# Attention followed by an affine MLP on one core: k's first two heads loaded apart, q's second pair turned after the first scores, row work put further back

## The chip, the cores and the metric

The kernel runs on one core of one Trainium2 chip. The core has five engines that take their instructions each from its own queue, in order: TensorE (PE, with its weight loads shown apart as PEld), VectorE (DVE), ScalarE (ACT), GpSimd (POOL) and SyncE (SP). SyncE, ScalarE and GpSimd also issue DMA transfers. The metric is device time in microseconds. Three runs of the kernel before took 739.56, 739.91 and 741.48 us, the median being 739.91 us.

## The reference

Eight batches of grouped-query attention (16 query heads, 4 key and value heads, sequence 384, head dimension 64) feed a residual MLP over 1024 channels. Cut to what matters:

```python
k, v = np.repeat(k, 4, axis=1), np.repeat(v, 4, axis=1)
scores = np.matmul(q, k.transpose(0, 1, 3, 2)) / np.sqrt(64)
attn = softmax(scores)                       # over the last axis
x = np.matmul(attn, v).transpose(0, 2, 1, 3).reshape(8, 384, 1024)
a1 = alpha1 * x + beta1
tok = np.einsum('ts,bsd->btd', w_tok, a1)    # mixes tokens
u = x + lam * tok
a2 = alpha2 * u + beta2
out = u + lam * (np.maximum(a2 @ w_ch1, 0.0) @ w_ch2)   # 1024 -> 4096 -> 1024
```

Inputs and output are float32; the kernel multiplies in bfloat16.

## The kernel before

The bulk of the time goes to the channel MLP, whose weights stream through a ring of six chunks. The first two batches are done one by one (`main`), the other six in pairs. While TensorE works on the MLP of one batch, the attention of the next is woven in between. Only batch 0 has nothing to hide behind: its attention (`side(0)`) stands alone at the start of the program, and the change lies there.

The order on each engine is written by hand: within `tc.manual_schedule` the instructions of every engine stand in the order of the Python calls, and semaphores are put in where data or a buffer is waited for. `side(0)` builds a list `us` of calls. At its head stand the turns of the first heads, then follow 18 groups of scores; the dictionary `at` says what comes behind group `i`. A group covers four of the 72 blocks (8 head pairs with 9 blocks each), so pair 1 comes in with group 2 and pair 2, which needs key heads beyond head 0, with group 4.

The steps that matter:

- `warmup(n)`: n matmuls on a zeroed tile, whose results nobody reads. Nine stand at the start, behind the memset of `wtokT` on VectorE; three come behind score group 0 and one behind group 3.
- `load_k`: heads 0 and 1 of k as one 192 KB load on SyncE's queue, followed by the row loads (`load_row`) of alpha1 and lam, then heads 2 and 3, then the other rows. q's first two pairs are two loads on ScalarE's queue, its other heads come through GpSimd.
- `place_k(0, 0, hs)`: casts a head of k to bfloat16 and writes it twice, one copy by VectorE and one by ScalarE; heads 2 and 3 are cast by GpSimd (`place_k(0, 1)`).
- `k_transpose` and `q_transpose`: TensorE turns a head or a pair into a PSUM tile, and VectorE (for q's first pair ScalarE) copies it to `kT` or `qT`. The PSUM tiles are named by tags: "tp" and "av" have one buffer each, "sc" (scores) and "mm" two each.
- `scores(i)`: four matmuls (two for each half of the array) into an "sc" tile, and the exponential of the whole tile on ScalarE.
- `av(p)`: the product with v for pair p; VectorE divides by the row sums (`rinv`, then `x`).
- `scale_rows`, `split`, `spread`, `a1`: the row vectors alpha1 and lam are multiplied, split in two bfloat16 parts on VectorE (five instructions on 32 partitions), spread by TensorE over all partitions ("vec") and copied to `g1`; `a1(p)` multiplies pair p with it.
- `wtok_transpose`, `rows_r`, `tok`: the token weights are turned, the vector R is made from them, and the token mix follows.

Of the kernel before, what the change touches and what calls it, by code (L numbers as in the profile page):

```python
# [12 lines left out]
def kernel(  # L13
# [21 lines left out]
    nc = tc.nc  # L35
    f32 = mybir.dt.float32
# [7 lines left out]
    B, Hq, S, D = q.shape  # L44
    Hkv = k.shape[1]
# [3 lines left out]
    P = 128  # L49
    NST = S // P  # L50
# [30 lines left out]
    hTf = hT.rearrange("p n s -> p (n s)")  # L81
# [45 lines left out]
    wtokT = const.tile([P, NST, S], bf, tag="wtokT", name="wtokT")  # L127
# [5 lines left out]
    ks, k2s, qrs = {}, {}, {}  # L133

    def by_head(ap):
        return ap.rearrange("h (p st) d -> p h st d", st=NST)

    def k_tile(b):
        k2s[b] = sb.tile([P, Hkv, 2, NST, D], bf, tag="k2", name="k2", bufs=1)

    def load_k(b, hs=(0, 2)):
        if b > 1:
            k_tile(b)
            for a in range(2):
                nc.gpsimd.dma_start(out=k2s[b][:, :, a], in_=by_head(k[b]))
            return
        for h in hs:
            ks[b, h // 2] = t = hTf[:, 7680 + 384 * h:8448 + 384 * h].bitcast(f32).rearrange(
                "p (h st d) -> p h st d", h=2, st=NST)
            nc.sync.dma_start(out=t, in_=by_head(k[b, h:h + 2]))  # L150

    def place_k(b, i, hs=(0, 1)):
        if b not in k2s:
            k_tile(b)
        copies = [nc.gpsimd.tensor_copy] * 2
        if b == 1 or b == 0 == i:
            copies = (nc.vector.tensor_copy, nc.vector.tensor_copy if i else nc.scalar.copy)
        lo, hi = hs[0], hs[-1] + 1
        for a in range(2):
            copies[a](out=k2s[b][:, 2 * i + lo:2 * i + hi, a], in_=ks[b, i][:, lo:hi])  # L160
# [22 lines left out]
    def load_w1(c):  # L183
        w1_slots[c] = w1_free.pop(0)
        nc.gpsimd.dma_start(out=w1[:, w1_slots[c]], in_=w1src[:, :, c * CW * P:(c + 1) * CW * P])  # L185
# [5 lines left out]
    def bank(shape, tag, name, dtype=f32):  # L191
        if tag == "mm":
            return mms.tile(shape, dtype, tag="mm", name=name, bufs=2)
        return psum.tile(shape, dtype, tag=tag, name=name, bufs=2 if tag == "sc" else 1)
# [34 lines left out]
    def side(b):  # L229
# [172 lines left out]
        def add(f, *a):  # L402
            us.append(lambda: f(*a))
# [28 lines left out]
        if not first:  # L432
# [10 lines left out]
            if (b - NPL) // 2 > 0:  # L443
                at = {}
# [18 lines left out]
                **{39 + 4 * i - i // 2 * 2: [(turn, p)] for i, p in enumerate((5, 6, 7)) if by_pe(p)}}  # L463
        add(k_transpose, 0, 1)
        add(q_transpose, 0, 1, "av", "ACT")
        add(place_k, 0, 0, (1,))
        add(q_transpose, 1, 1, "tp")
        lower, upper = range(NP // 2), range(NP // 2, NP)
        ut = a2_transpose
        at = {0: [(warmup, 3), (scale_rows, 0), (split, 0, 1, 0)], 1: [(k_transpose, 1, 1)],  # L470
              2: [(q_transpose, 2, 2, "av"), (split, 0, 1, 1)], 3: [(warmup, 1)],
              4: [(av, 0)], 5: [(spread, lower, "tp"), (a1, 0)], 6: [(av, 1), (k_transpose, 2, 2, "tp")],
              7: [(q_transpose, 4, 2, "av"), (a1, 1)], 8: [(av, 2)],
              9: [(wtok_transpose, 0, "av"), (wtok_transpose, 1, "tp")],
              10: [(wtok_transpose, 2, "av"), (q_transpose, 6, 2, "mm"), (fill_h, 0)], 11: [(av, 3), (rows_r, "tp")],
# [363 lines left out]
    with tc.manual_schedule(engines=order):  # L839

        def warmup(n):
            warm = bank([P, 512], "mm", "warm")
            for _ in range(n):
                nc.tensor.matmul(out=warm[:, :S], lhsT=wtokT[:, 0, :P], rhs=wtokT[:, 1, :],
                                 start=True, stop=True)

        nc.vector.memset(wtokT, 0.0)
        warmup(9)
        load_k(0, [0])

        rows_f = hTf[:32, 9216:10496].bitcast(f32)
        rows_t = hTf[:32, 10496:11520].bitcast(f32)
# [15 lines left out]
        def load_row(i, ap, n=4):  # L868
            nc.sync.dma_start(out=rows_f[:n * NP, i * P:(i + 1) * P],
                              in_=bass.AP(tensor=ap.tensor, offset=ap.offset, ap=[[0, n], [P, NP], [1, P]]))  # L870

        load_row(0, moe_alpha1)
        load_row(3, moe_lam)
        load_k(0, [2])
        load_row(1, moe_beta1)
        load_row(2, moe_alpha2, 1)
        load_row(4, moe_beta2, 1)
# [5 lines left out]
        def load_q4(g):  # L883
            nc.gpsimd.dma_start(out=qgs[g], in_=q[0, g * G:(g + 1) * G].rearrange("h (p st) d -> p h st d", st=NST))
# [5 lines left out]
            nc.vector.memset(t[:, :, :, D:], 1.0)  # L890
        AX = mybir.AxisListType.X
        nc.vector.tensor_copy(out=ident_f, in_=ident)
        for i, m in enumerate(masks):
            nc.vector.tensor_reduce(out=m, in_=ident[:32, 8 * (i + 1):24 + 8 * (i // 2)], op=ADD, axis=AX)
        nc.vector.tensor_scalar(out=masks[2], in0=masks[2], scalar1=-1.0, scalar2=None, op0=MUL)
# [47 lines left out]
        load_q4(2)  # L943
        nc.gpsimd.dma_start(out=wtok_in, in_=moe_w_tok.rearrange("(p tt) s -> p tt s", tt=NST))
        load_q4(3)
        place_k(0, 0, (0,))
        load_w1(order1[0])
        load_w1(order1[1])
        place_k(0, 1)
        scale_rows(1, nc.gpsimd)  # L950
        split(1, 2, None, nc.gpsimd)
# [6 lines left out]
            load_w2(0, r, h)  # L958
        for i, f in enumerate(side(0)):
            f()  # L960
            if i == 3:
                load_k(1)
        for i in range(3):
            rows4.append(sb.tile([P, 512], f32, tag="es", name="rows4", bufs=EB))
# [14 lines left out]
        def put_flips(ps, phase, b, places):  # L979
            for u, m in zip(places, ((flip_k, b), *((flip_q, b, i, 2) for i in range(0, NP, 2)))):  # L980
                put(ps, phase, u, *m)

        turns, at = side(1)
        put_all(0, 0, turns)
        put_all(0, 1, at)
        put_flips(0, 1, 2, (34, 36, 37, 42, 43))

        put(0, 1, 45, load_next, 3)
        put_all(1, 0, side(2)[1], lambda u: int(1.5 * u))
        put_flips(1, 0, 3, (53, 55, 57, 59, 61))  # L990
        put_all(1, 1, side(3)[1])
# [68 lines left out]
```

## Time and profile before

| what | value |
|---|---|
| median of three runs | 739.91 us |
| the profiled execution, its own time | 739.61 us |
| its span, first to last instruction | 737.8 us |
| TensorE busy | 727.0 us (99% of the span) |
| VectorE busy | 512.0 us (69%) |
| ScalarE busy | 325.7 us (44%) |
| GpSimd busy | 164.0 us (22%) |
| first matmul of k's turn | 4.38 us |
| first score matmul | 5.91 us |
| first exponential | 6.34 us |

The span counts from the first to the last instruction, and the remaining 1.8 us of the time lie around it. In a timeline a line gives start and duration in microseconds, the engine, the line of the code, the operation, output and inputs with their shapes, how many instructions were merged into the line, and in brackets the idle time of the engine ahead of it with what ended that idle time. A merged line spans from its first start to its last end, and consecutive instructions overlap by some hundredths of a microsecond, because an engine begins one while the one before drains. The matmul of a turn is short, and what its consumer sees is later by the way through the array.

### The profile page before, as it was taken

The page shows a single profiled execution, that of the slowest core. Times are in us where ns is not written, and L with a number is a line of the kernel's source. Part 1 is how long each engine was busy: PE and PEld are TensorE (multiplying, and loading weights), DVE is VectorE, ACT ScalarE, POOL GpSimd, SP SyncE. Part 2 cuts the span into 40 slices and gives each one's busy share as a digit, 9 for nine tenths or more (in the row PEclk, how much of TensorE's full clock was granted, in tenths as well). Part 3 has the DMA queues.
Part 4 walks back from the last instruction along what each step waited for, and adds up shares of the span by engine and source line. Part 5 has one row for each costly group of instructions (what it writes and reads, how often), then busy time and mean ns, then how long its engine had stood idle before and what let it go on. Part 6 is the DMA issues. An engine that isn't in the chain of part 4 may idle for free.

```text
span 737.8 us, 14477 instructions
## 1 busy us (share of the span) xinstructions
PE 727.0 (99%) x5710; PEld 418.6 (57%) x5769; DVE 512.0 (69%) x993; ACT 325.7 (44%) x469; POOL 164.0 (22%) x211
## 2 busy tenths in 40 slices
PE   8999999999999999999999999999999999999998
PEld 5866555666555566655555566655555556654444
DVE  7763366467587889749777988747958988762354
ACT  7632431554332566663334366664343266660000
POOL 9434221420000332301012244020002222000011
PEclk9999999999999999999999999999999999999999
DMA  9999999999999999999979999998989999837965
GB/s 188 194 202 200 207 217 179 186 198 181 219 264 260 183 226 223 249 262 215 284 186 224 178 176 165 190 250 199 276 236 167 217 149 144 149 136 241 289 184 107
DMA packets 218017, 151.31 MB, mean 205 GB/s; under 512 B 88661, under 2 KB 197061, under 8 KB 217949
## 3 DMA queue, kind: packets, MB, share of 16 engines
q0 software_dynamic: 120304, 64.60, 66.8%
q1 hardware_dynamic: 96956, 85.33, 41.5%
q8 instruction: 45, 0.74, 0.4%
q10 hardware_dynamic: 688, 0.46, 0.2%
q14 instruction: 24, 0.19, 0.1%
HBM read 154.84 MB, written 38.27 MB: 262 GB/s over the span
## 4 chain that ended last, share of the span: by engine, by line
PE 85%; DVE 6%; DMA 5%; issue 2%; POOL 2%; ACT 0%; DVEq 0%; POOLq 0%
PE C L789 25%; PE X L723 17%; PE h L532 10%; PE ch L570 10%; PE Y L723 8%; PE sc L279 4%; PE Z L723 4%; PE sc L315 3%; PE sc L340 3%; DMA q_raw<-in_q_dram 2%; DMA ops<-a 1%; DMA out_dram<-hT 1%; DVE xr L323 1%; DVE hT L826 1%; DVE xr L347 1%
## 5 line engine op out<-in xcount | busy, mean ns | idle before, releaser
L288 ACT ACTIVATE es<-sc 128x1024 bf16<-128x1024 f32 x126 | 121.4, 1024 | 154.6 <-PE sc L279 143.5
L789 PE MATMUL C<-w,arena 128*128 128x512 bf16 (+2 forms) x711 | 163.7, 372 | 1.6 <-issue 0.3
L789 PEld LDWEIGHTS <-arena 128*128 128x128 bf16 x1040 | 94.8, 98 | 100.5 <-issue 5.1
L728 ACT ACTIVATE hT<-X,bias 128x384 f32<-128x384 f32 x144 | 83.8, 582 | 63.8 <-PE X L723 56.8
L723 PEld LDWEIGHTS <-w 128*128 128x128 bf16 x768 | 75.1, 98 | 50.5 <-issue 0.7
L185 POOL DMA_DIRECT2D w<-in_moe_w_ch_dram x68 | 62.2, 926 | 125.4 <-PE Z L723 51.7
L570 PE MATMUL ch<-arena,hT 128*128 128x512 bf16 x366 | 87.9, 379 | 1.0 <-issue 0.3
L517 POOL DMA_DIRECT2D out_dram<-hT x33 | 28.8, 872 | 258.4 <-DVE hT L688 79.7
L532 PE MATMUL h<-ops,w 128*128 128x384 bf16 (+1 forms) x480 | 83.2, 327 | 0.4
L723 PEld LDWEIGHTS <-pad 128*128 128x128 bf16 x576 | 56.4, 98 | 37.2
L723 PE MATMUL X<-ops,w 128*128 128x384 bf16 x384 | 70.2, 326 | 0.0
L723 PE MATMUL X<-ops,pad 128*128 128x384 bf16 x384 | 70.2, 326 | 0.0
L789 PE MATMUL C<-pad,arena 128*128 128x512 bf16 (+2 forms) x288 | 69.5, 373 | 0.4
L532 PEld LDWEIGHTS <-w 128*128 128x128 bf16 x480 | 45.3, 98 | 30.1 <-issue 1.8
L570 PEld LDWEIGHTS <-hT 128*128 128x128 bf16 x384 | 34.7, 98 | 36.8 <-issue 2.5
L347 DVE TENSOR_TENSOR xr<-sc,xr 128x384 f32<-128x384 f32 x56 | 31.0, 553 | 24.2 <-PE sc L340 24.2
L315 PEld LDWEIGHTS <-es 128*128 128x128 bf16 x1008 | 38.2, 97 | 12.4
L340 PEld LDWEIGHTS <-wtokT 128*128 128x128 bf16 x576 | 37.5, 98 | 11.8 <-DVE a L330 0.8
L279 PE MATMUL sc<-qT,kT 64*128 64x384 bf16 (+2 forms) x576 | 41.9, 271 | 1.8 <-ACT hT L288 0.3
L320 DVE RECIPROCAL rinv<-sc 128x6 f32<-128x6 f32 x56 | 10.8, 192 | 44.3 <-PE sc L315 44.1
L315 PE MATMUL sc<-v,es 128*128 128x65 bf16 x1008 | 39.8, 193 | 0.0
L723 PE MATMUL Z<-ops,w 128*128 128x384 bf16 x192 | 39.0, 326 | 0.2
(138 smaller groups left out, 910.6 us busy)
## 6 DMA issues: line engine op xcount, KB each, us to landing
w<-in_moe_w_ch_dram POOLq DMA_DIRECT2D x68, 512.0 KB, 9.6
w<-w2s SPq DMA_DIRECT2D x60, 512.0 KB, 4.6
pad<-w2s SPq DMA_DIRECT2D x24, 512.0 KB, 7.4
out_dram<-xr SPq DMA_DIRECT2D x56, 192.0 KB, 5.3
out_dram<-hT POOLq DMA_DIRECT2D x33, 256.0 KB, 6.0
arena<-in_moe_w_ch_dram POOLq DMA_DIRECT2D x16, 512.0 KB, 20.0
w2s<-arena SPq DMA_DIRECT2D x28, 256.0 KB, 4.9
q_raw<-in_q_dram POOLq DMA_DIRECT2D x28, 192.0 KB, 9.7
```

The costliest lines, as they stand in the source:

```text
L185: nc.gpsimd.dma_start(out=w1[:, w1_slots[c]], in_=w1src[:, :, c * CW * P:(c + 1) * CW * P])
L279: nc.tensor.matmul(out=sc[:, hh, k % 4:k % 4 + n], lhsT=kT[r, 2 * p // G, BLK[hh][sk], :], rhs=qT[r, p, st:st + n, :], start=True, stop=True)
L288: nc.scalar.activation(out=e, in_=sc, func=EXP, scale=scale_qk)
L315: nc.tensor.matmul(out=av[:, hh, sq, :], lhsT=ess[k // 4][:, m % 2, k % 4, :], rhs=vb[:, sk, hk, :], start=(sk == 0), stop=(sk == NST - 1))
L340: nc.tensor.matmul(out=ps[:, tt, :], lhsT=wtokT[:, st, tt * P:(tt + 1) * P], rhs=a1s[p][:, st, :], start=(st == 0), stop=(st == NST - 1 an ...
L347: nc.vector.tensor_tensor(out=u, in0=ps, in1=u, op=ADD)
L517: nc.gpsimd.dma_start(out=at, in_=o, accum_op=ADD)
L532: nc.tensor.matmul(out=ps[:, :n], lhsT=w1[:, w1_slots[c], dt, j * P:(j + 1) * P], rhs=a2T[:, dt, :n], start=(dt == 0), stop=(dt == NDT - 1))
L570: nc.tensor.matmul(out=ps, lhsT=hT[:, nt, ms * P:(ms + 1) * P], rhs=w2[:, row(nt)[0], row(nt)[1], cs], start=(i == 0), stop=(i == NNT - 1))
L723: nc.tensor.matmul(out=ps, lhsT=tb[g, o][:, dt, e * P:(e + 1) * P], rhs=opb(LEFT1[o])[:, dt], start=(o in (1, 2, 7) and dt == 0), stop=(dt ...
L728: nc.scalar.activation(out=snap[o, e], in_=ps, func=IDENT, bias=hi if o == 5 else lo)
L789: nc.tensor.matmul(out=x, lhsT=hid[:, t, LEFT2[o], ms * P:(ms + 1) * P], rhs=rhs[:, t % 4 * 512 + c0:t % 4 * 512 + c1], start=((not last o ...
```

## The change

Five edits, all in the first batch's start:

1. `load_k` takes ranges of heads. Heads 0 and 1 become two loads of 96 KB, one right behind the other on SyncE's queue; heads 2 and 3 stay one load. The program has one DMA more.
2. The opening memset covers a third of `wtokT`, both operands of a warm-up come from that third, and eight warm-ups are issued in place of nine. The cast of head 0 stands on VectorE ahead of the small reductions that make the masks.
3. q's pair 1 is turned behind score group 0; in its old place, ahead of group 0, stand two warm-ups, and behind the turn of pair 1 one warm-up in place of three.
4. Head 1 of k is cast behind that turn, with both copies on VectorE (before, one was on ScalarE, ahead of the first exponential).
5. `scale_rows(0)` moves behind the turn of k's head 1, the whole of `split(0, 1)` behind the copy of q's third and fourth pairs (`q_transpose(2, 2)`), and `spread` of the first four pairs with `a1(0)` from behind group 5 to behind group 6, with the "av" tile in place of "tp". The load of the next batch's k is issued at the matching later point.

```diff
-    def load_k(b, hs=(0, 2)):
+    def load_k(b, parts=((0, 2), (2, 4))):
 ...
-        for h in hs:
-            ks[b, h // 2] = t = hTf[:, 7680 + 384 * h:8448 + 384 * h].bitcast(f32).rearrange(
-                "p (h st d) -> p h st d", h=2, st=NST)
-            nc.sync.dma_start(out=t, in_=by_head(k[b, h:h + 2]))
+        t = hTf[:, 7680:9216].bitcast(f32).rearrange("p (h st d) -> p h st d", h=Hkv, st=NST)
+        ks[b, 0], ks[b, 1] = t[:, :2], t[:, 2:]
+        for lo, hi in parts:
+            nc.sync.dma_start(out=t[:, lo:hi], in_=by_head(k[b, lo:hi]))
 ...
-            copies = (nc.vector.tensor_copy, nc.vector.tensor_copy if i else nc.scalar.copy)
+            copies = (nc.vector.tensor_copy, nc.vector.tensor_copy if i or hs == (1,) else nc.scalar.copy)
 ...
         add(k_transpose, 0, 1)
         add(q_transpose, 0, 1, "av", "ACT")
-        add(place_k, 0, 0, (1,))
-        add(q_transpose, 1, 1, "tp")
+        add(warmup, 2)
 ...
-        at = {0: [(warmup, 3), (scale_rows, 0), (split, 0, 1, 0)], 1: [(k_transpose, 1, 1)],
-              2: [(q_transpose, 2, 2, "av"), (split, 0, 1, 1)], 3: [(warmup, 1)],
-              4: [(av, 0)], 5: [(spread, lower, "tp"), (a1, 0)], 6: [(av, 1), (k_transpose, 2, 2, "tp")],
+        at = {0: [(q_transpose, 1, 1, "tp"), (place_k, 0, 0, (1,)), (warmup, 1)], 1: [(k_transpose, 1, 1), (scale_rows, 0)],
+              2: [(q_transpose, 2, 2, "av"), (split, 0, 1)], 3: [(warmup, 1)],
+              4: [(av, 0)], 6: [(spread, lower, "av"), (a1, 0), (av, 1), (k_transpose, 2, 2, "tp")],
 ...
-                nc.tensor.matmul(out=warm[:, :S], lhsT=wtokT[:, 0, :P], rhs=wtokT[:, 1, :],
+                nc.tensor.matmul(out=warm[:, :S], lhsT=wtokT[:, 0, :P], rhs=wtokT[:, 0, :],
 ...
-        nc.vector.memset(wtokT, 0.0)
-        warmup(9)
-        load_k(0, [0])
+        nc.vector.memset(wtokT[:, 0, :], 0.0)
+        warmup(8)
+        load_k(0, ((0, 1), (1, 2)))
 ...
-        load_k(0, [2])
+        load_k(0, ((2, 4),))
 ...
         nc.vector.tensor_copy(out=ident_f, in_=ident)
+        place_k(0, 0, (0,))
 ...
-        place_k(0, 0, (0,))
 ...
-            if i == 3:
+            if i == 5:
                 load_k(1)
```

## The prediction

> **What bounds the kernel now.** I read the page's busy shares first, then the start cut into windows, then TensorE's waits, then the start's timeline.
>
> ```profile
> PE 727.0 (99%) x5710; PEld 418.6 (57%) x5769; DVE 512.0 (69%) x993; ACT 325.7 (44%) x469; POOL 164.0 (22%) x211
> ```
>
> ```profile
> 0.00:20.00 20.00, 17.69 (x221) 10.97 (x221) 15.58 (x48) 15.63 (x19) 18.28 (x34) 1.00 1.25 189
> 20.00:42.00 22.00, 21.84 (x264) 16.69 (x261) 16.97 (x37) 11.83 (x22) 9.26 (x13) 1.00 1.46 197
> ```
>
> Columns of the windows: stretch, its length, then busy time of PE, PEld, DVE, ACT and POOL, granted clock, DMA share, GB/s. PE is idle 2.3 us of the first 20 and 0.2 us of the next 22; 99% holds after that. So the kernel is a block of TensorE work that begins near 20 us: an edit of the start is worth what it shifts that block, microsecond for microsecond, since no later wait on a transfer could give it back. TensorE's waits from 5 to 20 us:
>
> ```profile
> PE sc L279 <- ACT hT L288: 0.3, 1, 0.3
> PE tp L369 <- DVE wtokT L372: 0.2, 1, 0.2
> PE tok L344 <- DVE arena L387: 0.2, 1, 0.2
> ```
>
> The later two (at 15.56 and 19.21 in the timeline) are waits for VectorE. The beginning, by start, duration, engine:
>
> ```profile
> 1.52 3.06 PE L844 MATMUL warm<-wtokT 128*128 128x384 bf16 x9 [1.52 <-DVE wtokT L847]
> ...
> 4.38 0.53 PE L255 MATMUL tp<-ident,k 128*128 128x128 bf16 x3
> ...
> 4.70 1.20 PE L265 MATMUL tp<-hT,arena 128*128 128x128 f32 x6
> ...
> 5.91 0.39 PE L279 MATMUL sc<-qT,kT 64*128 64x384 bf16 x4
> ...
> 6.34 11.34 ACT L288 ACTIVATE hT<-sc 128x1024 bf16<-128x1024 f32 x12 [0.23 <-PE sc L279]
> ```
>
> Twelve exponentials follow each other with hardly a gap (11.34 / 12 = 0.945 each), so ScalarE sets a pace. But VectorE has none to spare either:
>
> ```profile
> 7.20 0.28 DVE L903 TENSOR_TENSOR hT<-hT 32x128 f32<-32x128 f32 x1 [0.70 <-DMA hT<-in_moe_lam_dram]
> 7.51 0.65 DVE L911 CAST hT<-hT 32x128 bf16<-32x128 f32 x1
> 8.20 0.48 DVE L913 SCALAR_TENSOR_TENSOR hT<-hT,arena 32x128 f32<-32x128 bf16 x1
> 8.61 0.34 DVE L257 COPY kT<-tp 128x384 bf16<-128x384 bf16 x1
> 8.88 0.53 DVE L267 COPY qT<-tp 128x768 bf16<-128x768 bf16 x1
> 9.34 0.22 DVE L911 CAST hT<-hT 32x128 bf16<-32x128 f32 x1
> 9.59 0.47 DVE L913 SCALAR_TENSOR_TENSOR hT<-hT,arena 32x128 f32<-32x128 bf16 x1
> 10.10 0.36 DVE L919 CAST hT<-hT 32x128 bf16<-32x128 f32 x1
> 10.43 0.20 DVE L320 RECIPROCAL rinv<-av 128x6 f32<-128x6 f32 x1
> ```
>
> After the wait for lam's row (0.70) it runs without a noted gap until 15.92, and it releases both late waits of PE. From 7 us on I therefore follow VectorE's queue.
>
> **The change part by part.**
>
> *Smaller memset, eight warm-ups.* The memset (0.93, 0.54 us for 576 columns) shrinks to 192; between the rows of 256 columns (0.27) and 4 columns (0.06) that is 0.22, so PE begins at 1.20, not 1.52. Nine warm-ups took 4.38 - 1.52 = 2.86, 0.32 each; one fewer lets k's transposes start at 4.38 - 0.32 - 0.32 = 3.74.
>
> *Head 0's own load.* Its 192 KB load let the casts go at 3.87. The trace has no 96 KB load here. Bounds: 0 gained (all fixed time), or 0.65 us (96 KB less at 150 GB/s, half of the 298 GB/s that the DMA view shows for 2.5 to 3.0 us, since q's load runs beside it). I take 0.45, nearer the upper row because both loads are in flight: 3.42. ScalarE's cast (0.35) ends at 3.77; k's transposes start at 3.80, not 4.38. The Trainium skill (DMA: Bandwidth & Descriptors, "Anatomy of one DMA") puts a load at about 2.0 us plus bytes over 436 GB/s; half the load would by that, as an estimate, gain only 0.23 us, and the sum below would be +0.6 instead of +0.5.
>
> *q's first pair.* Its transposes stand 0.32 behind k's: 4.12. But q's load, issued at 0.73 with 3.4 us to landing, comes at 4.13 to 4.2. That is what is late next; I take 4.20 against 4.70. Copy to ScalarE 0.68 behind before, 0.74 with all three at the slow rate of that time: 4.94. Scores 0 follow 0.53 later (5.47, before 5.91), exp 0.43 later: **5.90, 0.44 earlier**. The two new warm-ups stand in front of scores 0 while PE waits for that copy: nothing.
>
> *Second pair behind scores 0, head 1's casts on VectorE.* Scores 0 hold PE 0.33, so the pair's transposes start at 5.80; VectorE's copy came 0.58 behind theirs (5.35 to 5.94): 6.38, where before it was 5.94. Head 1's casts lay in the idle time at 5.22 (VectorE, 0.25) and 5.75 (ScalarE); now both queue behind that copy: 6.90 to 7.37. k's second transposes (7.15 before) need them; scores 2 are queued behind these on PE: 7.64, before 7.42. Exp 2 starts at 8.07 against 8.18, so **of 0.44 only 0.11 is left**.
>
> *Rows behind the third pair's copy.* kT's copy can follow at 7.80, lam's product at 8.10 (its row, one issue later on SyncE, about 7.6, no longer waits: the 0.70 goes). The third pair's transposes follow scores 2 at 7.97, its copy at 8.55 to 9.08. Then all of split: 0.76 for the first cast and product if the cast costs 0.22 as at 9.34, 1.19 if 0.65 as at 7.51; and 1.12 for the rest (9.34 to 10.46). I take 0.76: at 7.51 POOL was issuing weight loads, which end at 8.96. So the reciprocal of av 0 comes at 10.93, not 10.43: **VectorE is 0.5 late** (0.9 at the other end).
>
> *Spread one group later.* Scores 6 wait for exp 4, which now ends near 10.91; spread follows at 11.28 and its copy can start about 11.73. VectorE is ready at 10.93 + 0.70 = 11.63; before, the copy began at 11.14. Late by 0.6. The chain of VectorE behind it is full, so the copy of q's pairs 4 and 5 ends at 14.64, not 14.04; scores 9 (14.15, done 14.54, exp 9 at 14.71: 0.17 slack) slip to 14.75. The token weights' copies and R, which PE waits for at 19.21, follow 0.5 late.
>
> *Edits at nothing.* One more issue on SyncE (0.28 to 0.46): the row loads and k's heads 2 and 3 land that much later; POOL casts heads 2 and 3 at 8.90, as its own two weight issues end (8.96), not when they land. The masks (2.96 to 3.63 before) go behind head 0's cast, 3.68 to 4.35; the kT copy wants VectorE just then (before, it waited 0.81). The next batch's k is issued when head 1 is cast (7.4 instead of 6.13); it is used at 33.27. POOL's own order is unchanged. If any of these covers is gone, its price is that of the row: 0.1 to 0.4.
>
> **Sum.** -0.44 at the first exp, +0.33 at scores 2, then VectorE +0.5 past ScalarE's old pace, little of which PE's slack returns: **+0.5 us**, with ends -0.4 (start kept whole) and +0.9. The profiled execution took 739.61 us (span 737.8, and 1.8 around it), so 740.1 in its terms; the median of the runs shown, 739.91, is 0.3 above it, so I forecast 740.4.
>
> **Rivals.**
>
> *The start is kept (faster).* If VectorE reaches the reciprocal of av 0 by 10.0 and spread does not wait for scores 6, PE's block moves with the first exp: -0.44, 739.5. For it: 0.70 of idle goes and the slow cast (0.65) may be a 0.22. Against: 0.47 of casts and a copy 0.44 later enter the same queue. It decides at 10.43.
>
> *Head 0 lands no sooner.* The change does not do what it says; exp 0 near 6.3, and the rest of the chain as above: +0.9, 740.8. For: issue and completion may be most of the 3.1 us.
>
> *TensorE's clock opens later.* Three transposes took 0.53 at 4.38 and 0.34 at 7.15; in between the clock doubled, after 3.5 us of work without a gap (the clock column, 1.00 throughout, does not show it). Now PE has one warm-up fewer, transposes with a wait for q ahead of scores 0, and an idle 0.7 us before k's second transposes. If the step comes 3.4 us later, some 1.7 us of work is added, of which the 0.7 idle takes part: about +0.9 over the sum, +1.4, 741.3; twice as late, about +2.3, 742.2. The runs shown reach 741.48, which such a delay could be. The Trainium skill (TensorE: Matmul & The Clock Gate, "Part 1: The HAM clock gate") says that a free-running window of about 3.4 us must be busy before the clock opens, and "Part 4: PE-mode transpose" that transposes don't count as busy in the same way; by that rule a window ending near 5 us would now hold counted work up to 3.74 only. The trace agrees on the length, and shows nothing on transposes.
>
> **How the numbers follow.** VectorE's chain as worked out: 0.50 (own range 740.0 to 740.9). Start kept: 0.17. No sooner: 0.10. Clock later: 0.18, a third of it twice. Unforeseen: 0.05. A measurement here tells about 0.3% (2.2 us) from no change. None but the doubly late clock reaches that by itself; with the runs' own spread of 1.9 us I give slower 0.15 (0.06 twice late, 0.05 once late, 0.04 unforeseen), faster 0.05 (from the kept start), within 0.80. The range 739.2 to 742.2 leaves out the low half of the kept start and the tail above the doubly late clock.
>
> **What would show it.** Right: first exp near 5.9, k's second transposes waiting for VectorE's cast of k, no wait for lam's row, av 0's reciprocal near 10.9, PE's wait for R near 19.7. Wrong: av 0's reciprocal at or before 10.4 (kept start); warm-ups at 0.32 and transposes at 0.53 beyond 5.5 us (clock); head 0's cast at 3.8 (load).

## The result, and the profile after

The kernel after took 741.55 us in the median of 22 runs (740.45 to 744.39), the kernel before 739.88 us in 22 runs beside them: a ratio of 1.0023, 95% interval [1.0016, 1.0029]. Measured again on another occasion it was 741.01 against 739.98 us, 1.0013 [1.0005, 1.0022]. So the two medians put the cost at 1.7 and 1.0 us, and both intervals lie above 1: a real loss, but within the 0.3% that the prediction called no change. The forecast was 740.4 us with a range of 739.2 to 742.2.

The profiled execution took 741.19 us. From the first page of the kernel after:

```profile
span 739.4 us, 14535 instructions
...
PE 731.8 (99%) x5768; PEld 419.0 (57%) x5768; DVE 511.1 (69%) x994; ACT 325.6 (44%) x468; POOL 163.7 (22%) x211
```

The same two windows as before (stretch, length, busy time of PE, PEld, DVE, ACT, POOL, granted clock, DMA share, GB/s):

```profile
0.00:20.00 20.00, 17.06 (x195) 9.98 (x195) 14.46 (x44) 14.29 (x17) 18.20 (x33) 1.00 1.24 184
20.00:42.00 22.00, 21.83 (x278) 17.12 (x277) 16.59 (x40) 12.89 (x24) 9.29 (x13) 1.00 1.47 197
```

In the first 20 us PE is busy 17.06 us, where it was 17.69; ScalarE is busy 1.3 us less and VectorE 1.1 less. What PE waited for between 3 and 60 us:

```profile
PE tp L255 <- DVE k L160: 0.8, 1, 0.8
PE sc L279 <- DVE qT L267: 0.6, 2, 0.4
PE tp L369 <- DVE wtokT L372: 0.3, 1, 0.3
PE tok L344 <- DVE arena L387: 0.2, 1, 0.2
```

The wait for the exponentials (0.3 before) is gone; in its place stand waits for VectorE: its cast of k's head 1 and its copies of q. The timeline of the start (start, duration, engine, line, operation):

```profile
1.12 2.74 PE L843 MATMUL warm<-wtokT 128*128 128x384 bf16 x8 [1.12 <-DVE wtokT L846]
...
3.66 0.53 PE L255 MATMUL tp<-ident,k 128*128 128x128 bf16 x3
...
3.98 0.85 PE L265 MATMUL tp<-hT,arena 128*128 128x128 f32 x3
...
5.40 0.61 PE L279 MATMUL sc<-qT,kT 64*128 64x384 bf16 x4
...
5.94 0.90 PE L265 MATMUL tp<-hT,arena 128*128 128x128 f32 x3
6.04 1.02 ACT L288 ACTIVATE hT<-sc 128x1024 bf16<-128x1024 f32 x1 [0.71 <-PE sc L279]
...
6.88 0.56 DVE L267 CAST qT<-tp 128x384 bf16<-128x384 f32 x1 [2.29 <-PE tp L265]
...
7.05 1.82 POOL L185 DMA_DIRECT2D w<-in_moe_w_ch_dram  x2
7.35 0.90 DVE L160 CAST k<-hT 128x192 bf16<-128x192 f32 x2
...
8.14 0.45 PE L255 MATMUL tp<-ident,k 128*128 128x128 bf16 x3 [0.77 <-DVE k L160]
...
8.79 1.04 POOL L160 CAST k<-hT 128x384 bf16<-128x384 f32 x2
...
8.90 1.08 DVE L903 TENSOR_TENSOR hT<-hT 32x128 f32<-32x128 f32 x1
...
9.91 0.54 DVE L267 COPY qT<-tp 128x768 bf16<-128x768 bf16 x1
...
11.98 0.18 DVE L320 RECIPROCAL rinv<-av 128x6 f32<-128x6 f32 x1
```

The start is won and then lost. k's turn comes at 3.66 (before 4.38), the first exponential at 6.04 (6.34). Then the two casts of head 1 take 0.90 us together, k's second turn slips from 7.15 to 8.14, lam's product takes 1.08 us instead of 0.28, and the reciprocal of av 0 comes at 11.98 instead of 10.43. From there the whole block is late: PE's wait for the vector R ends at 20.71 (19.21), and the MLP's first matmul starts at 28.27 (26.76). The table follows the delay through the program; the last milestone ahead of the end is the first matmul of the first pair's stage.

| later than before by | R (us) | first MLP matmul | q's turn of batch 1 (50 us) | first pair's stage (242 us) | end |
|---|---|---|---|---|---|
| profile of after | 1.50 | 1.51 | 1.12 | 1.12 | 1.58 |

Between 51 and 242 us the delay stays at 1.12. But 0.39 is given back between 28 and 51 us, near 40 us as is shown below, and 0.46 is added past 242 us.

### The profile page after: what moved, and what is told of

It is laid out like the page before. It is cut to its first block, busy times and chain, and to the rows that moved or that the text cites. A ratio compares the mean times of both kernels' runs of the same rounds, so it can differ in the third digit from the quotient of the medians.

```text
span 739.4 us, 14535 instructions
## 1 busy us (share of the span) xinstructions
PE 731.8 (99%) x5768; PEld 419.0 (57%) x5768; DVE 511.1 (69%) x994; ACT 325.6 (44%) x468; POOL 163.7 (22%) x211
## 4 chain that ended last, share of the span: by engine, by line
PE 91%; DVE 6%; DMA 1%; issue 1%; ACT 0%; DVEq 0%
PE C L788 27%; PE X L722 17%; PE h L531 10%; PE ch L569 10%; PE Y L722 8%; PE sc L279 4%; PE Z L722 4%; PE sc L315 4%; PE sc L340 3%; DMA ops<-a 1%; PE h L223 1%; DVE hT L825 1%; PE tok L340 1%; DVE xr L323 1%; DVE xr L347 1%
## 5 line engine op out<-in xcount | busy, mean ns | idle before, releaser
L788 PE MATMUL C<-w,arena 128*128 128x512 bf16 (+2 forms) x744 | 168.4, 372 | 0.0
L569 PE MATMUL ch<-arena,hT 128*128 128x512 bf16 x384 | 90.8, 379 | 0.0
L320 DVE RECIPROCAL rinv<-sc 128x6 f32<-128x6 f32 x56 | 10.7, 191 | 44.4 <-PE sc L315 44.2
```

Source lines behind the costliest of these rows:

```text
L569: nc.tensor.matmul(out=ps, lhsT=hT[:, nt, ms * P:(ms + 1) * P], rhs=w2[:, row(nt)[0], row(nt)[1], cs], start=(i == 0), stop=(i == NNT - 1))
L788: nc.tensor.matmul(out=x, lhsT=hid[:, t, LEFT2[o], ms * P:(ms + 1) * P], rhs=rhs[:, t % 4 * 512 + c0:t % 4 * 512 + c1], start=((not last o ...
```

## The experiments

Four causes were on the table: the order itself (VectorE's and PE's queues, as the prediction had it), GpSimd slowing VectorE's casts, TensorE's clock, and the end of the program with one DMA more. Times of the single kernels' profiles are from the trace; "clock opens" is the moment at which the trace's own record of the granted clock goes from half to full. Each median is of 11 or 12 runs (of 22 for after, of five for weights later). The intervals reach 0.6 to 0.9 us to either side for those of 11 and 12, so most of these medians do not differ clearly from each other, and the milestones of the profiles have to tell. A profile shows one run.

| kernel | median / median of before beside it (us) | ratio [95%] | clock opens | R | first MLP matmul | 242 us to end |
|---|---|---|---|---|---|---|
| before | | | 5.00 | 19.21 | 26.76 | 495.86 |
| after | 741.55 / 739.88 | 1.0023 [1.0016, 1.0029] | 6.82 | 20.71 | 28.27 | 496.32 |
| loads and warm-ups alone | 740.39 / 739.99 | 1.0005 [0.9996, 1.0014] | 6.33 | 19.14 | 26.70 | 496.28 |
| order alone | 740.84 / 739.99 | 1.0008 [0.9999, 1.0017] | 4.63 | 20.05 | 27.59 | 495.91 |
| casts ahead | 740.61 / 739.99 | 1.0004 [0.9994, 1.0013] | 3.87 | 20.75 | 28.30 | 496.31 |
| rows back | 740.66 / 739.99 | 1.0009 [0.9998, 1.0021] | 7.15 | 23.20 | 30.76 | 496.33 |
| weights later | 744.23 / 740.08 | 1.0048 [1.0035, 1.0061] | 4.03 | 19.86 | 27.42 | 496.29 |
| product behind copy | 740.87 / 740.08 | 1.0011 [1.0002, 1.0019] | 6.33 | 20.63 | 28.18 | 496.30 |
| before, four warm-ups | 740.37 / 740.08 | 1.0003 [0.9994, 1.0012] | 9.72 | 20.66 | 28.21 | 495.86 |
| pair behind alone | 740.54 / 740.08 | 1.0006 [0.9997, 1.0015] | 3.78 | 19.42 | 26.96 | 496.26 |
| after again | 741.01 / 739.98 | 1.0013 [1.0005, 1.0022] | 5.22 | 19.87 | 27.41 | 496.31 |
| after, same count | 740.98 / 739.98 | 1.0014 [1.0005, 1.0023] | 7.10 | 22.05 | 29.60 | 495.88 |
| loads and warm-ups, same count | 740.41 / 739.98 | 1.0004 [0.9995, 1.0012] | 9.55 | 20.92 | 28.47 | 495.85 |
| next k whole | 740.19 / 739.90 | 1.0005 [0.9996, 1.0014] | 3.94 | 19.09 | 26.65 | 495.92 |

**Loads and warm-ups alone** (edits 1 and 2 on the kernel before):

```diff
+        nc.vector.memset(wtokT[:, 0, :], 0.0)
+        warmup(8)
+        load_k(0, ((0, 1), (1, 2)))
 ...
+        place_k(0, 0, (0,))     # head 0's cast ahead of the masks
```

> Edits 1 and 2 alone (split load, small memset, eight warm-ups, early cast of head 0); the order behind them is that of the kernel before. Theory A (the order of VectorE's queue and what GpSimd does beside it is what costs): the first exponential comes at 5.8 to 6.0 instead of 6.34 and nothing is paid for it, 739.3 to 739.7 us, ratio 0.9993 to 1.0000. Theory B (TensorE's clock opens later because of fewer and earlier warm-ups): the two transposes of q still run at the slow rate, 740.4 to 741.0 us, ratio 1.0007 to 1.0015.

Measured: first exponential 6.12, av 0's reciprocal 10.24, R 19.14, q's turn of batch 1 0.43 sooner than before, and yet the end at 737.78 against 737.83. A gain of 0.43 to 0.47 is there until 242 us (241.50 against 241.97) and gone at the end. It is not won at the start itself: the first MLP matmul is only 0.06 sooner, and the rest is won at 39 us, where VectorE gets the rows of lam at 38.72 instead of 39.09. The median, 740.39, shows no gain and is where the theory of the clock had it; the profiled run was the fastest of its twelve. So these two edits do not lose the time by the start.

**Order alone** (edits 3 to 5 on the kernel before):

```diff
-        add(place_k, 0, 0, (1,))
-        add(q_transpose, 1, 1, "tp")
+        add(warmup, 2)
 ...
-        at = {0: [(warmup, 3), (scale_rows, 0), (split, 0, 1, 0)], 1: [(k_transpose, 1, 1)],
+        at = {0: [(q_transpose, 1, 1, "tp"), (place_k, 0, 0, (1,)), (warmup, 1)], 1: [(k_transpose, 1, 1), (scale_rows, 0)],
 ...
-              4: [(av, 0)], 5: [(spread, lower, "tp"), (a1, 0)], 6: [(av, 1), (k_transpose, 2, 2, "tp")],
+              4: [(av, 0)], 6: [(spread, lower, "av"), (a1, 0), (av, 1), (k_transpose, 2, 2, "tp")],
```

> Edits 3, 4 and 5 alone, with the one load of 192 KB, the full memset and nine warm-ups of the kernel before. Theory A: the first exponential stays at about 6.3, the casts of head 1 and the row product meet GpSimd's instructions as they do in the changed kernel, and there is no head start to pay with: 741.3 to 742.0 us, ratio 1.0019 to 1.0029. Theory B: nine warm-ups open the clock at about 5.0 as before, so only the queue of VectorE is left: 740.3 to 740.7 us, ratio 1.0005 to 1.0011.

Measured: both casts of head 1 take 0.25, lam's product 0.37; the reciprocal comes at 11.21, the first MLP matmul 0.83 late. Theory A's stretched casts did not appear here. With head 1's casts undisturbed and the clock open by 4.63, the order still costs 0.8 us at the start: the mechanism of the forecast exists by itself. (Head 0's cast took 0.46 in this run, 0.26 in before, and puts k's first turn at 4.57 instead of 4.38.)

**Casts ahead** (after, head 1 cast before scores 0, one copy on ScalarE):

```diff
         add(q_transpose, 0, 1, "av", "ACT")
+        add(place_k, 0, 0, (1,))
         add(warmup, 2)
-        at = {0: [(q_transpose, 1, 1, "tp"), (place_k, 0, 0, (1,)), (warmup, 1)], ...
+        at = {0: [(q_transpose, 1, 1, "tp"), (warmup, 1)], ...
```

> The changed kernel with the casts of k's head 1 back ahead of the first scores, one on VectorE and one on ScalarE. Theory A: k's second turn starts near 7.3 instead of 8.14, VectorE gains the two casts (0.74 and 0.24) back, 740.2 to 740.7 us, about 1 us under the changed kernel. Theory B: the casts are not the cause, 741.2 to 741.7 us as the changed kernel.

Measured: k's second turn at 6.51 and the first exponential at 5.42, one of the two earliest of the study. Then PE runs into another transfer; its longest wait from 3 to 22 us:

```profile
PE av L315 <- DMA v<-in_v_dram: 1.4, 1, 1.4
```

PE began av 0 at 8.71 and then stood until the last part of v had landed, past 10 us; the clock closed from 10.70 to 14.11, and R came at 20.75. Without the casts behind scores 0 their delay is gone (0.25 on VectorE and 0.35 on ScalarE), but in this run the start could not be pulled further than v allowed.

**Rows back** (after, with lam's product, the halves of split and spread where before has them):

```diff
-        at = {0: [..., (warmup, 1)], 1: [(k_transpose, 1, 1), (scale_rows, 0)],
-              2: [(q_transpose, 2, 2, "av"), (split, 0, 1)], 3: [(warmup, 1)],
-              4: [(av, 0)], 6: [(spread, lower, "av"), (a1, 0), (av, 1), ...
+        at = {0: [..., (warmup, 1), (scale_rows, 0), (split, 0, 1, 0)], 1: [(k_transpose, 1, 1)],
+              2: [(q_transpose, 2, 2, "av"), (split, 0, 1, 1)], 3: [(warmup, 1)],
+              4: [(av, 0)], 5: [(spread, lower, "tp"), (a1, 0)], 6: [(av, 1), ...
```

> The changed kernel with the row work back where it was: scale_rows and the first half of split behind the turn of q's second pair, the rest behind the third pair's copy, spread behind group 5 in the tp tile. Theory A: the row product no longer meets GpSimd's casts of k (0.28 instead of 1.08), but it and half of split stand ahead of the copy of k's second turn; about 0.5 us gained, 740.8 to 741.3 us. Theory B: no change, 741.2 to 741.7 us.

Measured: the profiled execution was the slowest of its twelve, 743.33 us, and can't be set against the others; its clock closed from 10.56 to 17.39. But it shows one thing at its clearest, in the timeline of that kernel:

```profile
7.07 1.81 POOL L185 DMA_DIRECT2D w<-in_moe_w_ch_dram  x2
...
7.35 1.69 DVE L160 CAST k<-hT 128x192 bf16<-128x192 f32 x2
```

Two casts that take 0.25 each otherwise (0.742 and 1.026 here) stretch over GpSimd's two weight issues. The median, 740.66, is between the two kernels; what the place of the row work is worth is not settled by this run.

**Weights later** (after, with GpSimd's first two weight issues behind its casts and row work):

```diff
-        load_w1(order1[0])
-        load_w1(order1[1])
         place_k(0, 1)
 ...
-        for c in order1[2:RING]:
+        for c in order1[:RING]:
```

> The changed kernel with GpSimd's first two weight loads issued behind its casts and its row work, not ahead of them. Port theory (VectorE's cast of head 1 took 0.74 instead of 0.25 because GpSimd issued a weight load at that moment): the cast takes 0.25, k's second turn starts near 7.65 instead of 8.14; GpSimd's own casts come earlier and the row product may still meet them: 0.4 to 0.8 us under the changed kernel, 740.7 to 741.2 us. Queue theory (the length of VectorE's queue alone counts): cast as long as before, 741.2 to 741.7 us.

Measured: the first cast 0.249 (6.45), the second 0.59 beside another GpSimd issue, lam's product 0.28, the reciprocal at 10.95, R at 19.86. VectorE keeps the forecast's time here (10.93). But the clock opened at 4.03, and the unchanged order, in a run whose clock opened at 5.22 (after again, below), has the reciprocal at 11.11 and R at 19.87: this run does not separate GpSimd's issues from the clock. And the kernel is 0.5% slower, from a place past the start:

```profile
PE h L531 <- DVE hT L542: 3.1, 1, 3.1
```

GpSimd's memset of the rows for batch 1 came at 37.58 instead of 33.93, VectorE waited for those rows, PE for VectorE at 44.2 us, and the clock closed for one window. There is a transfer behind the start on which a later wait hangs; the prediction had excluded one.

**Product behind copy** (after, lam's product behind the copy of the third pair, away from GpSimd's casts):

```diff
-        at = {..., 1: [(k_transpose, 1, 1), (scale_rows, 0)],
-              2: [(q_transpose, 2, 2, "av"), (split, 0, 1)], ...
+        at = {..., 1: [(k_transpose, 1, 1)],
+              2: [(q_transpose, 2, 2, "av"), (scale_rows, 0), (split, 0, 1)], ...
```

> The changed kernel with the row product (scale_rows) moved from ahead of the third pair's copy to right behind it. Port theory: behind the copy GpSimd's casts of k are over, so the product takes 0.28 and the copy starts near 9.4 instead of 9.91; 0.5 to 0.8 us under the changed kernel, 740.6 to 741.1 us. Queue theory: the copy gains 0.3 at most and the row work is as late as before, 741.2 to 741.6 us.

Measured: the copy started at 9.23 instead of 9.91, and the product took 0.27 at 9.71, both as the port theory had it, and the median is in that theory's range. Yet the reciprocal came at 11.89, only 0.09 sooner than in after, and R at 20.63 against 20.71. The second cast of head 1 was again 0.745. Of the 0.68 that the copy won, the product, now behind it, takes 0.3 back, and the five instructions of split, which run from 10.02 to 11.89 beside GpSimd's own row work, take 0.27 us longer than in after (10.38 to 11.98).

**Before, four warm-ups** (five fewer):

```diff
-        warmup(9)
+        warmup(4)
```

> The kernel before with four warm-ups in place of nine, all else kept: TensorE stands idle from about 2.8 to 4.2 us and the clock should open later, near 7 to 10 us. Clock theory (a late clock costs the kernel time): 0.5 to 1.7 us slower than the kernel before, 740.4 to 741.6 us. Against it: ScalarE's pace covers the slow matmuls and the time is that of the kernel before, 739.7 to 740.2 us.

Measured: the clock opened at 9.72, the first exponential came at 7.00, and PE, out of warm-ups, stood until head 0's cast, which took 0.519 beside a GpSimd issue (0.260 in before), was done at 4.51:

```profile
PE tp L255 <- DVE k L160: 1.6, 1, 1.6
```

Head 1's cast took 0.608. The first MLP matmul was 1.45 late, the end 1.01. So a clock as late as this, with the stretched casts beside it, can produce the size of after's loss in before's order too. The median moved by only 0.29 us (ratio 1.0003 [0.9994, 1.0012]). That other runs open sooner would explain it; it is not shown, since only the profiled run shows its opening.

**Pair behind alone** (edits 1 and 2, with q's second pair behind scores 0; casts and row work as in before):

```diff
-        add(q_transpose, 1, 1, "tp")
+        add(warmup, 2)
-        at = {0: [(warmup, 3), (scale_rows, 0), (split, 0, 1, 0)], ...
+        at = {0: [(q_transpose, 1, 1, "tp"), (warmup, 1), (scale_rows, 0), (split, 0, 1, 0)], ...
```

> Edits 1 and 2 with q's second pair turned behind the first scores, but the casts of head 1 and all row work where the kernel before has them. If the casts and the row work are what costs, the head start is kept as far as v's landing (about 9 us) allows: 739.3 to 739.9 us. If turning the pair later costs by itself (its copy 0.4 to 0.9 later in VectorE's queue), 740.4 to 740.9 us.

Measured: exponentials 0 to 2 are 0.9 sooner than in before (5.39, 6.36, 7.28), the reciprocal is 0.17 later (10.60), R 0.21 later. VectorE's timeline says where the 0.9 us went:

```profile
7.33 0.28 DVE L904 TENSOR_TENSOR hT<-hT 32x128 f32<-32x128 f32 x1 [0.91 <-DMA hT<-in_moe_lam_dram]
7.65 0.41 DVE L912 CAST hT<-hT 32x128 bf16<-32x128 f32 x1
```

With the casts out of its queue, VectorE waits 0.91 for lam's row, and the copies of k and of q's third pair stand behind the row work (8.36 and 8.62): PE waits 0.58 for the latter. Then av 0 waits another 0.25 for v, until 9.91, and VectorE 0.21 for av 0. A start that is won by 0.9 us is not kept by this order either, and here it is transfers, lam's row and then v, that end it, not the casts.

**After again, and the number of DMAs.** Three kernels on one chip: after itself; after with k's heads 1 to 3 in one load; and the loads and warm-ups with the same merge.

```diff
-        load_k(0, ((0, 1), (1, 2)))
+        load_k(0, ((0, 1), (1, 4)))
 ...
-        load_k(0, ((2, 4),))
```

> The kernel after, unchanged, beside the two that follow. Both theories: 741.0 in the median, 740.5 to 742.6. If TensorE's clock is opened by a window that runs free of the program, the clock opens at another time than 6.82 us in this profile, and the first exponential, which lies ahead of it in both, stays within 0.1 us of 6.04 unless the clock opens ahead of 3.7 us. If the opening time follows from the order of the program's matmuls, it is 6.8 again.

> The kernel after with k's head 0 as one load and heads 1 to 3 as one, so that the program has as many DMAs as before. Theory of the semaphores' order: the stretch from the first pair's stage (242 us) to the last instruction takes 495.9 us as in before, 0.4 less than the 496.3 of after, because the last store's landing is again checked last and not third; 740.6 in the median. Rival, that the 0.4 at the end comes with the late start and not with the number of DMAs: 496.3 stays, and the median stays at 741.0. Head 1 lands with a load of 288 KB, some 0.6 us later than now, but ahead of 7.3, so the head's casts do not move.

> The loads and warm-ups alone (order of before), with heads 1 to 3 in one load, so as many DMAs as before. Theory of the semaphores' order: 0.4 under the same kernel with one DMA more, 740.0 against 740.4, no more than 0.1 from before. If head 1 now lands later than 5.2 us, its casts and k's second turn go back by as much, up to 0.5 us, which the rows of lam at 39 us hide in part. Rival: 740.4, as with one DMA more.

The profile of after again is the most telling of the study: the same program, with the clock open at 5.22. Its timeline:

```profile
5.39 0.40 PE L279 MATMUL sc<-qT,kT 64*128 64x384 bf16 x4
...
5.71 0.55 PE L265 MATMUL tp<-hT,arena 128*128 128x128 f32 x3
...
6.30 0.56 DVE L267 CAST qT<-tp 128x384 bf16<-128x384 f32 x1 [1.72 <-PE tp L265]
6.33 0.79 POOL L883 DMA_DIRECT2D qg<-in_q_dram  x1
...
6.77 0.59 DVE L160 CAST k<-hT 128x192 bf16<-128x192 f32 x2
...
7.26 0.45 PE L255 MATMUL tp<-ident,k 128*128 128x128 bf16 x3 [0.51 <-DVE k L160]
...
8.02 0.27 DVE L903 TENSOR_TENSOR hT<-hT 32x128 f32<-32x128 f32 x1
...
8.81 1.02 POOL L160 CAST k<-hT 128x384 bf16<-128x384 f32 x2
...
11.11 0.18 DVE L320 RECIPROCAL rinv<-av 128x6 f32<-128x6 f32 x1
```

Up to scores 0 (5.39 against 5.40) the two executions agree. Then the pair's turn takes 0.55 us instead of 0.90, VectorE copies it at 6.30 instead of 6.88, and GpSimd meets other instructions: the first cast takes 0.43, not 0.74, and lam's product is done before GpSimd's casts begin. So with a clock that opens 1.60 later the reciprocal came 0.87 later. This execution missed its expectation on one point (the first exponential came at 5.82, not near 6.04, since scores 0 straddle the opening); that the opening time is not fixed by the program was shown.

The count of DMAs shows in the stretch past 242 us: 495.88 and 495.85 with before's number, 496.31 with one more. Over the fourteen profiles the column splits without exception, 495.85 to 495.92 against 496.26 to 496.33. In the timeline it is the time from the last store's issue to the end of the span. Of before (span 737.83), after (739.41) and after with the same count (740.20):

```profile
735.33 0.37 ACTq L799 DMA_DIRECT2D out_dram<-ends  x1
```

```profile
736.48 0.37 ACTq L798 DMA_DIRECT2D out_dram<-ends  x1
```

```profile
737.70 0.36 ACTq L798 DMA_DIRECT2D out_dram<-ends  x1
```

That is 2.50, 2.93 and 2.50 us. The trace's semaphore events show why: at the end SyncE checks the landing semaphores one by one, some 0.06 us each, in a fixed order. The issues of SyncE and ScalarE take eight of these semaphores in rotation. Before has 304 such issues, and its last store has the semaphore that is checked last; after has 305, its last store has the first of the eight, and seven more checks stand behind its landing: 0.43 us. The medians did not fall with it (740.98 against 741.01, 740.41 against 740.39), though 740.6 and 740.0 were expected. The fastest runs did, 739.97 against 740.35 and 739.11 against 739.59, but these are single runs, the last two of different occasions. The merged load brings head 1 later (cast at 5.71 instead of 4.50 in the second kernel), and the clock differed from run to run, so the gain in the median is not shown.

**Next k whole** (loads and warm-ups alone, with the DMA saved at the next batch's k instead):

```diff
-                load_k(1)
+                load_k(1, ((0, 4),))
```

> The loads and warm-ups alone, with the next batch's k, which is first used past 33 us, as one load, so that the program has as many DMAs as before and nothing of batch 0 moves. Theory of the semaphores' order: X0 to the last instruction is 495.9 us, and at the same opening time of the clock as in loads_warmups_alone (6.33) the span is 737.4, 0.4 under before's 737.8. The fastest runs are near 739.1 and the median near 740.0, from 740.4 with one DMA more and 740.0 of before. Rival, that a gain at the start is lost in the rows of lam at 39 us whatever the end: the fastest run is at 739.5 and the median at 740.4.

Measured: 495.92 past 242 us as expected, the first MLP matmul at 26.65, and the median 740.19 against 739.90, between the two that were expected; the fastest run, 739.65, is nearer the rival's 739.5 than 739.1. Its profile was held up by three transfers. PE's waits, from 3 to 60 us and from 60 to 260 us:

```profile
PE tp L265 <- DMA arena<-in_q_dram: 0.9, 1, 0.9
PE h L532 <- DVE hT L543: 0.9, 1, 0.9
```

```profile
PE h L532 <- DMA ops<-a: 1.4, 1, 1.4
```

The first is q's second pair, the second hangs on the rows of lam for batch 1, the third ends at 134.6 us, where neither before nor after has such a wait. So the comparison of spans at a like clock, which was expected, did not come about. No kernel of this study is shown to beat the kernel before.

## Why the prediction was right, and where its terms were off

The class and the range held; the size did not. The sum said +0.5 us, and the two comparisons of medians gave +1.7 and +1.0. The first of them, 741.55, lies beyond the 740.0 to 740.9 of the main chain and near the 741.3 of the clock rival. That it is so near is in part luck: as is shown below, the clock did take part, but so did a term at the program's end that the sum had at nothing.

*VectorE's chain: right.* The prediction's milestones against after again, whose clock opened near before's (5.22 and 5.00):

| step | predicted | after again | after |
|---|---|---|---|
| first exponential | 5.90 | 5.82 | 6.04 |
| exponential 2 | 8.07 | 8.07 | 8.96 |
| lam's product | 8.10 | 8.02 | 8.90 |
| reciprocal of av 0 | 10.93 | 11.11 | 11.98 |
| copy behind spread | 11.73 | 11.79 | 12.67 |
| scores 9 | 14.75 | 14.79 | 15.64 |
| R | 19.7 | 19.87 | 20.71 |

The named signs came: k's second turn waits for VectorE's cast, lam's row is waited for no longer. The start is not kept in either profile: the reciprocal is beyond 10.43 in both.

*Head 0's own load: right in sign, too small.* The casts went at 2.98, not 3.42: 0.89 sooner, more than the upper bound of 0.65. The rival that it lands no sooner is out. The formula of the Trainium skill (DMA: Bandwidth & Descriptors, "Anatomy of one DMA") had given 0.23; that section is about loads through GpSimd, this one goes through SyncE, and the traces do not agree with the formula here: by the semaphore events the last bytes landed at 3.84 in before and at 2.95 in after. q's first load, named as late next, was not: it landed at 3.50 instead of 4.17, and its pair turned at 3.98 without a wait, predicted 4.20. Scores 0 still came at 5.40 against 5.47, because the copy began 0.88 behind the first of the three turns at half clock, where the prediction had 0.74.

*TensorE's clock: the rival took part.* It was priced at +0.9 over the sum. Between the two profiles of after the later opening is worth 0.86 at the first MLP matmul and 0.63 at the end, near that price. The sign that the prediction named for it came in the first profile: the pair's turn at 5.94 is still at the slow rate (0.90). Its cause was wrongly argued: the same program opened at 5.22 and at 6.82, so the run decides, and one warm-up fewer is not needed for it. Whether the fewer warm-ups also change how often it opens late is not shown; nine were profiled twice (5.00 and 4.63). The fourteen openings lie between 3.78 and 7.15 us but for 9.55 and 9.72, a spread of about one period of 3.41 us, and every stretch between two changes of the clock in the traces is a whole number of such periods. The Trainium skill says this (TensorE: Matmul & The Clock Gate, "Part 1: The HAM clock gate": a window that runs free of the program, so that the opening varies from run to run), and the traces agree. The prediction left open whether turns count as work for the clock. Here they did: the window from 3.41 to 6.82 us of after opened it with at most 2.10 us of other matmuls in it (1.49 of warm-ups, 0.61 of scores), while one with PE busy for 2.61 us, nearly all warm-ups, had not (rows back, 0.32 to 3.73).

What the change did is make the start sensitive to it. With edits 3 to 5, and no second closing before it, R comes at 19.86 to 20.05 where the clock opens at 4.03 to 5.22, and at 20.63 to 20.71 where it opens at 6.33 and 6.82; the loads and warm-ups with before's order have R at 19.14 with 6.33 and at 19.09 with 3.94 (next k whole). The pair's float32 turn and k's second turn now stand behind each other on the path, and at half clock they push VectorE into GpSimd's work.

*The clock closes again, which no rival had.* A window of 3.41 us at half clock lowers a run's mean clock to 0.998. Of the 22 first runs of after seven have that value, and these took 742.09 to 742.64 us; the other fifteen took 740.45 to 741.90 but for one of 744.39. One of 12 has it in after again, three of 12 in the version with the same count, whose profiled execution (741.98 us) shows it: the clock is closed from 10.51 to 13.93. None of 105 runs of before made beside the experiments has it. Without these runs the two medians of after are 741.08 (of 15) and 741.00 (of 11), 1.2 and 1.0 us above before: the different share of such runs explains most of why one comparison gave 1.7 us and the other 1.0.

A sign of what closes it stands in the windows of the starts: the three behind which it closed had PE busy for 1.87 to 2.14 of 3.41 us, while the lowest behind which it stayed open had 2.44 (pair behind alone, 7.20 to 10.61), after 2.57 (6.82 to 10.24) and before 3.31 (5.00 to 8.41). In the version with the same count PE's two waits for head 1's casts, 0.65 and 0.62 us, lie in that window. So the waits that the new order brings in seem able to close the clock too. It is no sharp rule (near the end of the program, 733.86 to 737.27 in after, 1.76 did not close it), and where the clock closed in runs that were not profiled is not known.

*VectorE's durations: two terms mis-sized.* Head 1's casts were priced at 0.25 each and lam's product at 0.28. In the profile of after the first cast took 0.736 and the product 1.077, each while GpSimd was at work, 1.28 us together; the first also holds PE. The row of before that showed it (0.65 at 7.51) was read only for split. The Trainium skill says the rule (SBUF — State Buffer, "Who interferes with whom"): VectorE and GpSimd share a pair of ports, and where a VectorE instruction needs it, for its two-port mode or for a second input from SBUF, whoever comes second is blocked until the first is done. The traces agree in part. Lam's product, with two inputs, takes 0.27 to 0.37 where it ends before GpSimd's casts begin (after again, weights later, order alone) and 1.077 beside both of them. But in order alone both casts of head 1 began inside a GpSimd issue, 0.07 and 0.23 us behind its start, and still took 0.25; the last section has the counts.

*One more DMA at nothing: wrong, +0.43.* The issue cost nothing at the start, where it was looked for; it cost 0.43 at the program's end.

*"No later wait on a transfer could give it back": wrong.* At 40 us VectorE waits for rows of lam for batch 1. VectorE's timeline there, of before and of after:

```profile
39.09 0.01 DVE L931 LOAD_MASK_SELECT vecs<-rows  x1 [0.84 <-DMA rows<-in_moe_lam_dram]
```

```profile
39.68 0.01 DVE L931 LOAD_MASK_SELECT vecs<-rows  x1
```

VectorE is idle 0.84 us for them in before, in after not at all. A block that comes 1.51 later is 1.12 late beyond that place; and a faster start is kept only as far as the rows come sooner too. When they come does not follow the start: GpSimd's memset of their tiles, which stands ahead of their loads, came at 33.93 in before, 34.07 in after, and 33.05 in before with four warm-ups, whose block is 1.45 late. Past the rows, up to 242 us, the block of after is as rigid as predicted.

So at a like clock (after again against before): +0.65 at the first MLP matmul from VectorE's chain (predicted 0.5), -0.15 by 242 us, +0.45 past it, +0.95 at the end. With the clock opening late: +1.51, -0.39 and +0.46, which is +1.58. How often a run falls between these stays open, since only the profiled runs show their opening.

## What to carry to other kernels

A step that is moved to another place on VectorE is to be priced by what GpSimd does at that moment, not by its duration where it stood. When a start lies near the opening of TensorE's clock, an order in which several turns follow each other on the path makes the time depend on a moment that changes from run to run; look at more than one profile before a milestone is put down to the change. And count the DMAs that SyncE and ScalarE issue: one more can cost at the end of the program. A late transfer behind the start can cap what the start wins, or give back some of what it loses.

## What the runs showed of the hardware that was not expected

*GpSimd's DMA issue blocks VectorE mostly in its later part.* Of the 21 casts of k's head 1 (0.25 us, from float32) that VectorE made in the fourteen profiles, 13 began within 0.23 us of the start of a GpSimd issue, and eleven of these took 0.24 to 0.25; two took 0.93 and 1.03, both right behind a cast that had been held itself, as were two of the eleven. All seven that began 0.25 to 0.44 into an issue ended 0.08 to 0.11 after it, with up to 0.745. One that began 0.65 into an issue took 0.26. Why the start within an issue matters is not shown. So 0.1 us of shift can decide over half a microsecond of a cast's time.

*Half the bytes landed 0.9 us sooner.* The 192 KB load of two heads let the casts go at 3.87 us; the 96 KB load of one, issued at the same time with the other behind it, had landed by 2.96 to 3.05 in most profiles with the split load, where the casts start as their engines come free.

*The order of the checks at the end.* With eight landing semaphores in rotation, which of them the last store gets was worth 0.43 us of 740. The fourteen profiles split by the number of issues alone, whatever their order at the start.
